# Eight weight pieces get their low half from GpSimd's subtraction instead of an accumulating transfer, and builds of one-hot sets are charged anew

## The chip, the cores and the metric

The kernel runs on one core of a Trainium2 chip. A core has five engines that run their own instruction lists in order and wait for each other through semaphores: TensorE (PE, with its weight loads shown as PEld), VectorE (DVE), ScalarE (ACT), GpSimd (POOL) and SyncE (SP), which here only issues transfers. The metric is the device time of one execution in microseconds (us); lower is better. A profiled execution gives the start and the length of every instruction.

## The reference

For x of 2048 rows (tokens) by 640 columns the kernel computes a gated mix of two layers:

```python
g = sigmoid((x * gate_w).sum(-1, keepdims=True))
a = einsum("bsd,ed->bse", x, dft_hid_re)
b = einsum("bsd,ed->bse", x, dft_hid_im)
A = einsum("ts,bse->bte", dft_seq_re, a) - einsum("ts,bse->bte", dft_seq_im, b)
# B: product-key experts. q = x @ w_q, 32 heads x 2 halves of 128
# s1, s2 = scores of each half against 16 keys; the best 2 of each give 4 pairs,
# the best 2 of these name rows (16*i1 + i2) of u and v (256 x 640) and, by softmax, weights w
# B = sum over heads and the 2 picks of  w * gelu(x . u[row]) * v[row]
out = g * A + (1 - g) * B
```

All products are made as three float32r products of a high and a low half (the low half is the float32 value less its rounded high half), so each matrix that is multiplied has to be split into two tiles first.

## The kernel before

**What runs when.** TensorE works through one long list. Its backbone are 128 *pieces*: the sequence matrices `dft_seq_re` and `dft_seq_im` come as 2 x 4 *chunks* of 512 output rows, each of 16 pieces of 128x512. Piece n is multiplied with the 128 rows `X[s]` of x (5 column blocks d, 3 matmuls each, so 15 matmuls; `seq_piece`, L146 to L148). A chunk's five banks are copied out by ScalarE (L248), multiplied by the gate on VectorE (`gate_piece`, L220) and stored. Pieces 0 to 63 are the real part, 64 to 127 the imaginary one. Between the pieces stand the score products of the expert layer (up to piece 61), the expert blocks (below), and behind piece 127 the 84 steps of the last stage.

**How a piece is split.** `split_piece(n)` is called three pieces ahead, into one of four places of the tile `WS`. ScalarE rounds the loaded piece `wf` to the high half (L141 or L191). The low half comes in one of two ways. In the first, GpSimd subtracts: low = wf - high (L142). In the second, ScalarE writes minus the high half into the low half's place (L192), and GpSimd issues a transfer that reads the piece from memory again and accumulates it there (L194). The second way holds for pieces 34 to 63, and for the even ones of pieces 76 to 90, which are eight. All other pieces take the first way. The five `wf` buffers are loaded by SyncE five pieces ahead (L180). GpSimd also splits the hidden matrices into `DD` in this stretch (`split_dd`, 128x640, ten halves between pieces 72 and 94).

**The expert part.** VectorE finds the best keys of each token (`topk`, `gates`, `weights`); then `experts` turns them into tables of sums. For each of 32 sub-blocks (g, c) `build` makes a *set* of one-hot matrices `hot` with three VectorE instructions of 128x1024 in f16 (L875: two comparisons, one multiplication). `use` lets TensorE multiply a group of up to four sets, 32 small matmuls for each (L889): such a group of 128 matmuls is called a *block* here, and there are eight blocks in the program. The first matmul of each set waits for that set's third build instruction. Behind a block ScalarE masks the result (L826) and VectorE adds it up (L832). A set's place is built again once the block has read it. There are four places, later five.

**What sets the order.** The program is written out at build time. The VectorE work of the expert part comes out of a pump, `bg`: each group of three piece matmuls adds 0.95 x 0.68 us of credit (`run_bg`), and each step of the work takes its charge off. So a charge does not change how long an instruction runs; it decides behind how many piece matmuls the next step stands, and therefore where the blocks stand in TensorE's list. A build instruction is charged by L876:

```python
for o, a, b, op in ((pt, row(0), wt, OP.is_equal), (qt, row(1), wt, OP.is_equal), (pt, pt, row(2), OP.mult)):
    nc.vector.tensor_tensor(o, a, b, op=op)
    yield (0.9 if early else 1.05) + (settle() if op == OP.mult else 0.0)
```

`early` holds for pieces before 92 (NT is 16, NC is 4, so NT * (NC + 2) - 4 is 92). N0 is 30, and N1 is 66.

Of the kernel before, what the change touches and what calls it, by code (L numbers as in the profile page):

```python
# [13 lines left out]
OP = mybir.AluOpType  # L14
# [11 lines left out]
NT = S // P  # L26
NP = NT // 2
TC = 512
NC = S // TC
NPC = 2 * NC * NT  # L30
# [13 lines left out]
MS = 64 // TB  # L44
CG = P // (TB * E)
BYPASS = 4
ACCUM_END = NT * (NC + 2) - 4


class Pump:  # L50
# [59 lines left out]
def gated_mix_kernel(ctx: ExitStack, tc: tile.TileContext, xT, xn, dreT, dimT, wsre, wsim, wq, kT, uT, vv, gw, out):  # L110
# [28 lines left out]
    def split(f, h, l, eng):  # L139

        nc.scalar.activation(h, f, AF.Copy)  # L141
        eng.tensor_sub(l, f, h.bitcast(F32))  # L142
# [29 lines left out]
    N0 = 3 * NG + 6  # L172
# [11 lines left out]
    def split_piece(n):  # L184
        if n < NPC:
            psp[n] = h, l = WS[:, n % 4, 0], WS[:, n % 4, 1]
            f = pf.pop(n)
            if not N0 + 4 <= n < (4 * NT if n % 2 else ACCUM_END) or 4 * NT <= n < N1 + 10:
                split(f, h, l, nc.gpsimd)
                return  # L190
            nc.scalar.activation(h, f, AF.Copy)  # L191
            nc.scalar.activation(l, h.bitcast(F32), AF.Copy, scale=-1.0)  # L192
            w, c, s = pieces[n]
            nc.gpsimd.dma_start(l, (wsre, wsim)[w][c, s], accum_op=OP.add)  # L194
# [7 lines left out]
    def follow(n):  # L202
        for f in then.pop(n, ()):
            f()
# [3 lines left out]
    p3, last_part, ending, closing, early, late, share = None, False, False, False, True, False, 0.95  # L208
# [22 lines left out]
    def seq_piece(n):  # L231
        w, c, s = pieces[n]
        if s == 0:
            banks[:] = [bank(d) for d in range(KD)]
        load_piece(n + 5)
        split_piece(n + 3)
        h, l = psp.pop(n)
        if n < BYPASS:
            for a, (x, c) in enumerate(((0, h), (0, l), (1, h)) if n == 0 else ((0, h), (1, h), (0, l))):
                for d in range(KD):  # L240
                    nc.tensor.matmul(banks[d], X[s][:, x, d * P:(d + 1) * P], c, start=n + a == 0, stop=False)  # L241
            return
        for d in range(KD):
            ds = slice(d * P, (d + 1) * P)
            mm3(banks[d], X[s][:, 0, ds], X[s][:, 1, ds], h, l, s == 0, s == NT - 1)
            if s == NT - 1:
                staged[n // NT, d] = f = stage()
                nc.scalar.activation(f, banks[d], AF.Copy)  # L248
            run_bg(0.68)

    for q in range(2 * NC):
        n = NT * (q + 1)
# [85 lines left out]
    for n in (1, 2):  # L338
        split_x(n)
        split_piece(n)  # L340
# [163 lines left out]
    n = b + 2  # L504
# [277 lines left out]
    for p in range(NP):  # L782
        n = N0 + 4 * p + min((p + 1) // 2, 3)
        for a in range(4):
            at(n + 1 + a, score_step, p, a)
    N1 = n + 5
# [26 lines left out]
    def experts():  # L813
# [9 lines left out]
        def mask(t):  # L823
            f = t.rearrange("p m (e t) -> p (m e) t", t=TB)
            for n in range(TB):
                nc.scalar.activation(f[:, :, n], f[:, :, n], AF.Copy, scale=mask_t[:, n:n + 1])  # L826

        def add_up(g, c, t):
            if c == 0:
                store_gates(g - 1)  # L830
                cd[g] = p3.tile([P, E, P], F32, name="cd", tag="cd")
            nc.vector.tensor_reduce(cd[g][:, :, 8 * c:8 * c + 16].rearrange("p e m -> p m e"),  # L832
                                    t.rearrange("p m (e t) -> p m e t", e=E), op=OP.add, axis=AX.X)
            if c == 14:
                summed[g] = cd[g]

        def settle(force=False):
            us = 0.0
            if masked:
                add_up(*masked.popleft())  # L840
                us = 0.75
            if unmasked and (force or not closing):
                masked.append(unmasked.popleft())
                mask(masked[-1][2])
            return us
# [16 lines left out]
        def pair(s):  # L862
            f = HOT[s][1] if s == 4 else HOT[s]
            return f[:, 0], f[:, 1]

        def build(g, c, s):
            pt, qt = (f.rearrange("p (m e t) -> p m e t", e=E, t=TB) for f in pair(s))

            def row(n):
                r = ROWS[g][:, n, 8 * c:8 * c + 8, :].rearrange("p b (s t) -> p (b s) t", t=TB)  # L870
                return r[:, :, None, :].to_broadcast(shp)

            assert rowed >= set(range(8 * g, 8 * g + 8))
            for o, a, b, op in ((pt, row(0), wt, OP.is_equal), (qt, row(1), wt, OP.is_equal), (pt, pt, row(2), OP.mult)):
                nc.vector.tensor_tensor(o, a, b, op=op)  # L875
                yield (0.9 if early else 1.05) + (settle() if op == OP.mult else 0.0)  # L876

        def use(group):
            assert not last_part
# [15 lines left out]
        while todo or prev:  # L895
            group = []
            while todo and (len(group) < (2 if ending else 4) or len(group) % 2):
                free = free_now()
                if prev and (not free or ending and any(s in (2, 3) for g, c, s in prev)):
                    yield from use(prev)  # L900
                    prev = []
                    continue
                if not free:
                    break
                s = min(free) if ending else free[0]
                free_sets.remove(s)
                g, c = todo.popleft()
                group.append((g, c, s))
                yield from build(g, c, s)
            if prev:  # L910
                if not group:
                    yield 2.2
                yield from use(prev)
            prev = group
# [165 lines left out]
    for k, (n, m) in enumerate(((-1, 2), (0, 4), (5, 7), (7, 9), (10, 12))):  # L1080
        n, m = NT * (NC + 2) + n, NT * (NC + 2) + m
# [8 lines left out]
    def split_step(m):  # L1090
        if m < 2 * NSTEP:
            b, (u, k) = m // NSTEP, divmod(m % NSTEP, KZ)
            what = UNITS[u]
            key = (b, "s" if (b or k == KD) and what in ("s1", "s2", "s4") else what, k)
            sp[m] = ring(m)[:, 0], ring(m)[:, 1]
            split(raw[key], *sp[m], nc.vector if what in ("s2", "s3") else nc.gpsimd)
            bg.credit -= 0.8 if what in ("s2", "s3") else 0.0
            if what in ("a22", "s3", "s4") or k < KD and (b == 0 or what in ("a11", "a12")):
                give(key)
# [161 lines left out]
    prep_split = {NPC - 4: (0,), NPC - 3: (1,), NPC - 2: (2,), NPC - 1: (3, 4)}  # L1261
    WP = None
    for n in range(N0, NPC):
        ending, closing, early, late = n >= NPC - 7, n % NT == NT - 1, n < ACCUM_END, n >= NT * (NC + 2) - 10
        assert n < NT * (NC + 2) - 1 or not HOT[4:] or HOT[4][0] or 4 in free_sets
        seq_piece(n)
        follow(n)
        if n >= N1 and p3 is None and NT // NB - 1 in gated:
            p2_stack.close()
            p3 = ctx.enter_context(tc.tile_pool(name="p3", bufs=1, reuse_waits="tile"))  # L1270
            pools.append(p3)
            for t in ("hot0", "WP"):
                f = p3.tile([P, 2, 2, 16 * E * 4], F16, name="hot", tag=t)
                HOT.extend(f[:, a] for a in range(2))
            bg.add(experts(), late=True)
            bg.credit -= 3.0
        if n == NPC - 4:
            bg.drain(lambda: {2, 3} <= set(free_sets))
            HOT[2:4] = None, None
            WP = p3.tile([P, 2, 2, TC], F32R, name="WP", tag="WP")  # L1280
        for m in prep_split.get(n, ()):
            split_step(m)
# [54 lines left out]
```

## Time and profile before

| what | value |
|---|---|
| median of 3 runs | 749.75 us (749.32 to 749.88) |
| the profiled execution | 750.07 us, of which its span (first to last instruction) is 748.3 us |
| VectorE busy | 577.6 us (77%) |
| GpSimd busy | 345.1 us (46%) |
| ScalarE busy | 336.8 us (45%) |
| subtractions of pieces on GpSimd, L142 WS<-wf | 89, mean 1481 ns |
| accumulating transfers, L194 | 30 of the real part, 8 of the imaginary part; these 8 land 6.1 us after issue in the median |
| granted TensorE clock | 1.0 throughout |

A row of the timeline reads: start in us, length in us, engine, line of the kernel, operation, written tile <- read tiles, shapes, count. Rows of one line that follow each other are merged (x2), and a bracket at the end gives idle time of the engine just ahead and what ended it. A row of the waits reads: who waited, for whom, us in total, times, longest.

### The profile page before, as it was taken

What the parts mean: (1) busy time and instruction counts of PE and PEld (TensorE: products, weight loads), DVE (VectorE), ACT (ScalarE), POOL (GpSimd) and SP (SyncE); (2) the same over time, 40 slices, a digit from 0 to 9 for tenths busy, and PEclk for the clock granted to TensorE, in tenths of its full rate; (3) what the DMA queues carried; (4) which work ended last, traced back from release to release, by engine and by line L of the source; (5) the groups of instructions that cost most, each with busy time, mean ns of one, the idle gap of its engine ahead of it and who ended that gap; (6) DMA issues with size and microseconds to landing.
All of it is one profiled execution on the core that took longest, in us unless ns stands there. A gap on an engine that the chain in (4) does not pass through costs nothing.

```text
span 748.3 us, 12035 instructions
## 1 busy us (share of the span) xinstructions
PE 744.0 (99%) x4437; PEld 605.2 (81%) x4437; DVE 577.6 (77%) x722; ACT 336.8 (45%) x564; POOL 345.1 (46%) x286
## 2 busy tenths in 40 slices
PE   9999999999999999999999999999999999999998
PEld 7777777888888888888888887888888888888887
DVE  6874087595999899999999978987798883357651
ACT  4335234543544745555553574422334553443351
POOL 5543323640532424145245566634356693487253
PEclk9999999999999999999999999999999999999999
DMA  9999899788566686972498766388856788875302
GB/s 336 375 387 359 332 354 387 207 233 263 143 177 136 184 232 164 243 214 71 114 393 294 157 168 197 122 291 268 272 211 197 230 260 309 246 237 175 112 29 71
DMA packets 84491, 171.17 MB, mean 229 GB/s; under 512 B 16080, under 2 KB 21328, under 8 KB 84176
## 3 DMA queue, kind: packets, MB, share of 16 engines
q1 hardware_dynamic: 76000, 155.31, 61.4%
q0 software_dynamic: 5472, 9.96, 8.5%
q10 hardware_dynamic: 2960, 5.13, 1.9%
q8 instruction: 35, 0.57, 0.3%
q14 instruction: 24, 0.20, 0.1%
HBM read 136.40 MB, written 32.39 MB: 226 GB/s over the span
## 4 chain that ended last, share of the span: by engine, by line
PE 97%; DMA 1%; issue 0%; ACT 0%; POOL 0%; DVE 0%; ACTq 0%; POOLq 0%
PE b L146 31%; PE b L147 30%; PE b L148 30%; PE b L386 2%; PE b L241 2%; PE b L889 1%; DMA WS<-in_wsim 1%; PE b L332 1%; ACT rows L730 0%; POOL DD L142 0%; ACT b L826 0%; ACT DD L141 0%; DVE ST L1222 0%; ACT WS L141 0%; ACTq L141 0%
## 5 line engine op out<-in xcount | busy, mean ns | idle before, releaser
L146 PE MATMUL b<-WS,X 128*128 128x512 f32 x620 | 243.3, 392 | 0.0
L147 PE MATMUL b<-WS,X 128*128 128x512 f32 x620 | 241.7, 390 | 0.2 <-DMA WS<-in_wsim 0.2
L148 PE MATMUL b<-WS,X 128*128 128x512 f32 x620 | 241.5, 390 | 0.0
L142 POOL TENSOR_TENSOR WS<-wf,WS 128x512 fp32r<-128x512 f32 x89 | 131.5, 1481 | 174.8 <-ACT WS L141 172.8
L146 PEld LDWEIGHTS b<-WS,X 128*128 128x128 f32 x620 | 116.4, 188 | 28.1 <-issue 4.1
L148 PEld LDWEIGHTS b<-WS,X 128*128 128x128 f32 x620 | 116.5, 188 | 24.3
L147 PEld LDWEIGHTS b<-WS,X 128*128 128x128 f32 x620 | 116.5, 188 | 24.1 <-DMA WS<-in_wsim 0.7
L141 ACT ACTIVATE WS<-wf 128x512 fp32r<-128x512 f32 x89 | 55.5, 627 | 109.4 <-PE b L148 70.9
L875 DVE TENSOR_TENSOR hot<-rows,wtab 128x1024 f16<-128x1024 f16 x56 | 50.6, 940 | 14.4 <-PE b L889 14.4
L142 POOL TENSOR_TENSOR xl<-xf,xh 128x640 fp32r<-128x640 f32 x16 | 26.8, 1677 | 72.5 <-ACT xh L141 72.5
L573 ACT ACTIVATE sc<-b 128x512 f32<-128x512 f32 x32 | 19.5, 610 | 79.9 <-PE b L148 76.1
L194 POOL DMA_DIRECT2D WS<-in_wsre x30 | 26.4, 879 | 59.5 <-ACT WS L192 58.2
L142 POOL TENSOR_TENSOR WS<-ra,WS 128x512 fp32r<-128x512 f32 x33 | 46.6, 1422 | 15.3 <-ACT WS L141 10.4
L141 ACT ACTIVATE WS<-ra 128x512 fp32r<-128x512 f32 x47 | 29.4, 631 | 42.7 <-PE b L148 28.5
L631 DVE TENSOR_TENSOR eq<-sc,mm 128x1024 f16<-128x1024 f32 x32 | 44.2, 1383 | 0.9
L638 DVE TENSOR_REDUCE tied<-eq 128x64 f32<-128x1024 f16 x32 | 39.0, 1219 | 0.9
L629 DVE TENSOR_REDUCE mm<-sc 128x64 f32<-128x1024 f32 x32 | 38.7, 1210 | 0.2
L142 POOL TENSOR_TENSOR WP<-ra,WP 128x512 fp32r<-128x512 f32 x13 | 19.2, 1490 | 31.0 <-ACT WP L141 30.9
L220 DVE SCALAR_TENSOR_TENSOR ST<-ST,grow 128x512 f32<-128x512 f32 x40 | 32.3, 864 | 0.6 <-ACT ST L248 0.6
L147 PE MATMUL b<-WU,xh 128*128 128x512 f32 x80 | 31.2, 389 | 0.0
L148 PE MATMUL b<-WU,xl 128*128 128x512 f32 x80 | 31.2, 389 | 0.0
L146 PE MATMUL b<-WU,xh 128*128 128x512 f32 x80 | 31.1, 389 | 0.0
(214 smaller groups left out, 1435.7 us busy)
## 6 DMA issues: line engine op xcount, KB each, us to landing
X<-xd SPq DMA_DIRECT2D x36, 640.0 KB, 6.6
wq<-in_wq SPq DMA_DIRECT2D x32, 640.0 KB, 7.8
wf<-in_wsim SPq DMA_DIRECT2D x64, 256.0 KB, 5.0
wf<-in_wsre SPq DMA_DIRECT2D x63, 256.0 KB, 6.7
pd<-ST SPq DMA_DIRECT2D x40, 256.0 KB, 6.1
ra<-pd SPq DMA_DIRECT2D x40, 256.0 KB, 3.5
WS<-in_wsre POOLq DMA_DIRECT2D x30, 256.0 KB, 6.3
xd<-X SPq DMA_DIRECT2D x11, 640.0 KB, 9.1
```

The costliest lines, as they stand in the source:

```text
L141: nc.scalar.activation(h, f, AF.Copy)
L142: eng.tensor_sub(l, f, h.bitcast(F32))
L146: nc.tensor.matmul(o, wh, ah, start=first, stop=False, skip_group_check=more)
L147: nc.tensor.matmul(o, wh, al, start=False, stop=False, skip_group_check=more)
L148: nc.tensor.matmul(o, wl, ah, start=False, stop=last, skip_group_check=more)
L194: nc.gpsimd.dma_start(l, (wsre, wsim)[w][c, s], accum_op=OP.add)
L220: nc.vector.scalar_tensor_tensor(f, f, -1.0 if w else 1.0, g, op0=OP.mult, op1=OP.mult)
L573: copy = lambda o, f: nc.scalar.activation(o, f, AF.Copy)
L629: nc.vector.tensor_reduce(m, sc, op=OP.max, axis=AX.X)
L631: nc.vector.tensor_tensor(eq, sc, m[:, :, None].to_broadcast([P, HH, E]), op=OP.is_equal)
L638: nc.vector.tensor_reduce(tied[:, s, ib, :], eq, op=OP.add, axis=AX.X)
L875: nc.vector.tensor_tensor(o, a, b, op=op)
```

## The change

Three lines differ:

```diff
-ACCUM_END = NT * (NC + 2) - 4
+ACCUM_END = NT * NC
...
-            if not N0 + 4 <= n < (4 * NT if n % 2 else ACCUM_END) or 4 * NT <= n < N1 + 10:
+            if not N0 + 4 <= n < ACCUM_END:
                 split(f, h, l, nc.gpsimd)
                 return
...
-                yield (0.9 if early else 1.05) + (settle() if op == OP.mult else 0.0)
+                yield (1.05 if early else 0.9) + (settle() if op == OP.mult else 0.0)
...
-        ending, closing, early, late = n >= NPC - 7, n % NT == NT - 1, n < ACCUM_END, n >= NT * (NC + 2) - 10
+        ending, closing, early, late = n >= NPC - 7, n % NT == NT - 1, n < NT * (NC + 2) - 4, n >= NT * (NC + 2) - 10
```

The accumulating way now ends with piece 63, so the even pieces 76 to 90 are split like the others: ScalarE's second pass and GpSimd's issue go, a subtraction on GpSimd comes. `early` still ends at piece 92, but the two charges have changed places: 1.05 before it, 0.9 behind it.

On GpSimd, at pieces 76 to 80, each issue `L194` has become a subtraction at the same place of the list (`DD` are the halves of the hidden matrices):

```order
 L142 TENSOR_TENSOR DD<-draw,DD 128x640
-L194 DMA WS<-in_wsim 128x512
-L142 TENSOR_TENSOR WS<-wf,WS 128x512
+L142 TENSOR_TENSOR WS<-wf,WS 128x512 x2
 L142 TENSOR_TENSOR DD<-draw,DD 128x640
-L194 DMA WS<-in_wsim 128x512
-L142 TENSOR_TENSOR WS<-wf,WS 128x512
-L194 DMA WS<-in_wsim 128x512
+L142 TENSOR_TENSOR WS<-wf,WS 128x512 x3
 L142 TENSOR_TENSOR DD<-draw,DD 128x640
```

Eight issues fewer and eight subtractions more stand on GpSimd's list; nothing else on it has moved.

On TensorE, the first block of expert matmuls stood inside piece 79, behind its second column block (bank b1). Before:

```order
L146 MATMUL b1_3074<-WS_90,X_579 128x512
L147 MATMUL b1_3074<-WS_90,X_579 128x512
L148 MATMUL b1_3074<-WS_90,X_579 128x512
L889 LDWEIGHTS hot_3442
L889 MATMUL b5_3561<-hot_3442 32x32
```

Now it stands behind the fifth (bank b4), at the end of piece 79:

```order
L146 MATMUL b4_3077<-WS_90,X_579 128x512
L147 MATMUL b4_3077<-WS_90,X_579 128x512
L148 MATMUL b4_3077<-WS_90,X_579 128x512
L889 LDWEIGHTS hot_3441
L889 MATMUL b5_3569<-hot_3441 32x32
```

That is 9 large matmuls later. Counted in the same way, the eight blocks stand 9, 15, 24, 30, 33, 18, 3 matmuls later and, the last, 3 matmuls earlier. The number of TensorE instructions and of blocks is the same.

On VectorE, the list up to the end of the first group of four sets is the same. Behind it comes the second group (`hot_` tiles, `rows0` the key rows of the first half of the tokens), with the gate's five instructions and the sums of the first block (its banks b5 and b6). Before:

```order
L875 TENSOR_TENSOR hot_3442<-rows0_1217,wtab_159 128x1024 x2
L875 TENSOR_TENSOR hot_3442<-hot_3442,rows0_1217 128x1024
L875 TENSOR_TENSOR hot_3443<-rows0_1217,wtab_159 128x1024
L220 SCALAR_TENSOR_TENSOR ST_68<-ST_68,grow_3541 128x512 x5
L875 TENSOR_TENSOR hot_3443<-rows0_1217,wtab_159 128x1024
L875 TENSOR_TENSOR hot_3443<-hot_3443,rows0_1217 128x1024
L832 TENSOR_REDUCE cd_3788<-b5_3561 128x16x16
L875 TENSOR_TENSOR hot_3443<-rows0_1217,wtab_159 128x1024 x2
L875 TENSOR_TENSOR hot_3443<-hot_3443,rows0_1217 128x1024
L832 TENSOR_REDUCE cd_3788<-b6_3626 128x16x16
```

Now:

```order
L875 TENSOR_TENSOR hot_3441<-rows0_1217,wtab_159 128x1024
L220 SCALAR_TENSOR_TENSOR ST_68<-ST_68,grow_3536 128x512 x5
L875 TENSOR_TENSOR hot_3441<-rows0_1217,wtab_159 128x1024
L875 TENSOR_TENSOR hot_3441<-hot_3441,rows0_1217 128x1024
L832 TENSOR_REDUCE cd_3780<-b5_3569 128x16x16
L875 TENSOR_TENSOR hot_3442<-rows0_1217,wtab_159 128x1024 x2
L875 TENSOR_TENSOR hot_3442<-hot_3442,rows0_1217 128x1024
L832 TENSOR_REDUCE cd_3780<-b6_3634 128x16x16
L875 TENSOR_TENSOR hot_3442<-rows0_1217,wtab_159 128x1024 x2
L875 TENSOR_TENSOR hot_3442<-hot_3442,rows0_1217 128x1024
```

The gate falls into the group's second set instead of its third, and both sums stand ahead of the fourth set instead of around it.

## The prediction

> **What bounds the kernel now.** I read the busy shares first, then TensorE's waits, then its list in order of time.
>
> ```profile
> span 748.3 us, 12035 instructions
> PE 744.0 (99%) x4437; PEld 605.2 (81%) x4437; DVE 577.6 (77%) x722; ACT 336.8 (45%) x564; POOL 345.1 (46%) x286
> PE 97%; DMA 1%; issue 0%; ACT 0%; POOL 0%; DVE 0%; ACTq 0%; POOLq 0%
> PE b L332 <- PEq L1329: 0.8, 1, 0.8
> PE b L147 <- DMA WS<-in_wsim: 0.2, 1, 0.2
> ```
>
> TensorE sets the end, from start to finish. A busy row can hide a wait, since the ends of matmuls are modelled; but the waits hold two lines only, the launch and one transfer. So the first question is how much that transfer costs. TensorE's timeline around it:
>
> ```profile
> 452.64 0.39 PE L146 MATMUL b<-WS,X 128*128 128x512 f32 x1
> 453.26 0.50 PE L147 MATMUL b<-WS,X 128*128 128x512 f32 x1 [0.23 <-DMA WS<-in_wsim]
> 453.60 0.40 PE L148 MATMUL b<-WS,X 128*128 128x512 f32 x1
> 453.93 1.26 PE L889 MATMUL b<-hot 128*32 128x32 f16 x128
> ```
>
> Undisturbed matmuls start 0.23 us apart (rows further down). Here the steps are 0.62 and 0.34 us: 0.39 too long while the accumulated low half was late, and 0.11 on restarting. That is 0.5 us, and it is all that this change could win on TensorE, whose number of instructions stays the same. A forecast of a large gain would need another bound, and the profile has none. So the question is what the change makes TensorE wait for.
>
> **What goes.** Eight accumulating transfers and their issues on GpSimd, and eight second passes on ScalarE. Their only visible cost is that 0.5 us: -0.5 (between 0, if another wait would take its place at once, and -0.5). ScalarE is busy for 45% and on no path, so its passes of 0.63 us count as nothing; less memory traffic counts as nothing too, since no other transfer ends a wait of TensorE.
>
> **What comes: subtractions that hold up VectorE.** The two engines get in each other's way. VectorE's and GpSimd's timelines ahead of the first expert block:
>
> ```profile
> 343.11 0.29 DVE L690 TENSOR_TENSOR rp<-tied 128x128 f16<-128x128 f32 x1
> 404.12 1.27 DVE L690 TENSOR_TENSOR lb<-tied 128x128 f16<-128x128 f32 x1
> 409.66 2.38 DVE L875 TENSOR_TENSOR hot<-rows,wtab 128x1024 f16<-128x1024 f16 x2
> 411.96 0.68 DVE L875 TENSOR_TENSOR hot<-hot,rows 128x1024 f16<-128x1024 f16 x1
> 412.56 1.28 DVE L875 TENSOR_TENSOR hot<-rows,wtab 128x1024 f16<-128x1024 f16 x2
> 414.37 2.97 DVE L875 TENSOR_TENSOR hot<-rows,wtab 128x1024 f16<-128x1024 f16 x2
> 417.26 1.78 DVE L875 TENSOR_TENSOR hot<-hot,rows 128x1024 f16<-128x1024 f16 x1
> 420.17 0.68 DVE L875 TENSOR_TENSOR hot<-hot,rows 128x1024 f16<-128x1024 f16 x1
> 421.13 1.29 DVE L875 TENSOR_TENSOR hot<-rows,wtab 128x1024 f16<-128x1024 f16 x2 [0.28 <-PE b L889]
> ```
>
> ```profile
> 400.75 0.90 POOL L194 DMA_DIRECT2D WS<-in_wsim  x1 [1.26 <-ACT WS L192]
> 403.90 1.33 POOL L142 TENSOR_TENSOR WS<-wf,WS 128x512 fp32r<-128x512 f32 x1 [2.26 <-ACT WS L141]
> 407.55 0.89 POOL L194 DMA_DIRECT2D WS<-in_wsim  x1 [0.73 <-ACT WS L192]
> 409.96 1.53 POOL L142 TENSOR_TENSOR WS<-wf,WS 128x512 fp32r<-128x512 f32 x1 [1.53 <-ACT WS L141]
> 414.30 0.88 POOL L194 DMA_DIRECT2D WS<-in_wsim  x1 [2.81 <-DMA wf<-in_wsim]
> 414.90 1.88 POOL L142 TENSOR_TENSOR DD<-draw,DD 128x640 fp32r<-128x640 f32 x1
> 416.75 1.75 POOL L142 TENSOR_TENSOR WS<-wf,WS 128x512 fp32r<-128x512 f32 x1
> 421.10 0.90 POOL L194 DMA_DIRECT2D WS<-in_wsim  x1 [2.60 <-ACT WS L192]
> 438.59 1.28 POOL L142 TENSOR_TENSOR WS<-wf,WS 128x512 fp32r<-128x512 f32 x1 [0.86 <-ACT WS L141]
> ```
>
> An undisturbed set takes 414.37 - 412.56 = 1.81 us, so 0.60 for an instruction. The one at 417.26, with a subtraction running, takes 1.78 instead of 0.68: +1.10. The small L690 at 404.12, again with one running, takes 1.27 where the row at 343.11 has 0.29: +0.98. The first four sets end at 420.17 + 0.68 = 420.85, after 11.19 us; four times 1.81 is 7.24, and the other 3.95 fall on three GpSimd instructions (409.96, 414.90, 416.75): 1.32 each. The issue L194 at 421.10 costs nothing: the two builds beside it take 1.29, like the undisturbed 1.28.
>
> Which new subtractions stand ahead of the end of that group? Those in place of the four issues at 400.75, 407.55, 414.30 and 421.10 (pieces 76 to 82). The first and the last of ScalarE's four high halves for them:
>
> ```profile
> 399.04 0.63 ACT L191 ACTIVATE WS<-wf 128x512 fp32r<-128x512 f32 x1 [2.14 <-issue]
> ...
> 419.39 0.63 ACT L191 ACTIVATE WS<-wf 128x512 fp32r<-128x512 f32 x1 [2.72 <-PE b L148]
> ```
>
> They are ready at 399.67 and 420.02, so all four subtractions can start before the group's present end at 420.85, and the last falls among builds that are late already. And VectorE has nothing to catch up with: its waits between 300 and 421 us are this one line,
>
> ```profile
> DVE xf L459 <- POOL xl L142: 0.2, 1, 0.2
> ```
>
> so every delay there reaches the last build. I take 1.10 for the two among VectorE's small instructions and 1.32 for the two among the builds: 2 x 1.10 + 2 x 1.32 = 4.84 us. The ends: only the two among the builds cost, at 1.10 (2.2 us), or all four cost their whole length, 1.53 by the row at 409.96 (6.1 us). The value lies between, nearest to what the same group pays now.
>
> By the Trainium skill (SBUF — State Buffer, Who interferes with whom), GpSimd and a VectorE instruction with two SBUF inputs exclude each other, and whichever starts first keeps the shared ports for its whole instruction. By that rule each subtraction costs up to its undisturbed 1.28 us, 5.1 in all, and the forecast would be 0.3 us later; the row at 425.53 below, where GpSimd waits through several VectorE instructions, shows that the order of service is less simple than that.
>
> **What moves: the block.** The first block now stands 9 matmuls later, because its 12 builds are charged 0.15 more each. The rows:
>
> ```profile
> 419.64 0.39 PE L148 MATMUL b<-WS,X 128*128 128x512 f32 x1
> 420.32 0.39 PE L148 MATMUL b<-WS,X 128*128 128x512 f32 x1
> 420.64 1.26 PE L889 MATMUL b<-hot 128*32 128x32 f16 x128
> 421.83 0.50 PE L146 MATMUL b<-WS,X 128*128 128x512 f32 x1
> ```
>
> Three matmuls take 0.68, so nine take 2.04. The block takes 421.83 - 420.64 = 1.19, and its last quarter, which needs the fourth set, begins 0.89 after its start: at 421.53 now, 0.68 after the set is ready, and at 423.57 with the change. The set will be ready at 420.85 + 4.84 = 425.69. TensorE waits 2.1 us, plus 0.1 to restart: **+2.2**. No wait comes below a delay of 2.04 + 0.68 = 2.72 us; the upper end, 6.1, gives +3.5.
>
> **The blocks behind it.** The second now starts at 439.07:
>
> ```profile
> 425.53 5.55 POOL L142 TENSOR_TENSOR DD<-draw,DD 128x640 fp32r<-128x640 f32 x1 [3.53 <-ACT DD L141]
> 431.05 1.74 POOL L142 TENSOR_TENSOR WS<-wf,WS 128x512 fp32r<-128x512 f32 x1
> 439.07 1.26 PE L889 MATMUL b<-hot 128*32 128x32 f16 x128
> 439.56 1.47 DVE L875 TENSOR_TENSOR hot<-rows,wtab 128x1024 f16<-128x1024 f16 x2 [3.47 <-PE b L889]
> DVE hot L875 <- PE b L889: 14.4, 5, 4.7
> ```
>
> It moves by 15 matmuls (3.4 us) and the 2.2 of the wait, so its last quarter begins at 439.07 + 3.4 + 2.2 + 0.9 = 445.6. Its builds start at 425.69: 12 builds, the gate's 5 and 2 sums are 19 x 0.60 = 11.4, and some seven GpSimd instructions in that time (pieces 83 to 87, two halves of DD) cost 7.7 at 1.10 to 9.2 at 1.32: ready at 444.8 to 446.3. From 0.8 early to 0.7 late; I take 0. The third moves by 24 matmuls (5.4), so its last quarter begins at 453.93 - 0.5 + 5.4 + 2.2 + 0.9 = 461.9; its builds start when the second block has read its first set (445.0) and need 14 x 0.60 + 6 x 1.32 = 16.3, ready at 461.3: 0. Further on no accumulating transfer is replaced, and VectorE idles up to 4.7 us for the block (last line), against blocks that stand at most 15 matmuls, 3.4 us, closer together because of the charge of 0.9: 0.
>
> **The low halves themselves** come earlier: a subtraction of 1.3 to 1.7 us takes the place of a second pass and a transfer of some 6 us, so that wait goes for good.
>
> **The sum.** -0.5 + 2.2 = +1.7 us. The profiled execution took 750.07 (748.3 of span and 1.8 around it) and becomes 751.8; it lies 0.3 above the median of 749.75, which becomes 751.5, **+0.23%**.
>
> **The rivals.**
>
> *No wait comes, and the kernel is not slower.* The row at 425.53 speaks for it: GpSimd's 1.9 us of work took 5.55 because VectorE did not let it in. If GpSimd gives way like that to the builds, the four subtractions cost VectorE less than 2.72 us and the first block waits for nothing. Against it: in the eleven microseconds before, at 409.96, 414.90 and 416.75, GpSimd went first. Time: 749.75 - 0.5 = 749.25. Chance 0.27.
>
> *Three blocks wait.* At 1.53 for each GpSimd instruction the first waits 3.5, the second some 1.0 and the third 0.5; 749.75 - 0.5 + 5.0 = 754.3. Against it: only one of the rows is so dear. Chance 0.12.
>
> *GpSimd's list gets late instead.* Piece 83's low half is ready at 431.05 + 1.74 = 432.8, and its first use comes about 9 + 45 + 1 matmuls after 421.83 (the rest of piece 79, then three pieces), at 434.4: 1.6 us of room. If GpSimd is shut out longer than the 3.7 us of the row at 425.53 while one more subtraction is queued ahead, TensorE waits for the low halves of pieces 83 to 85, 1 to 3 us: about 751.5 in all. The wait at the first block would itself give 2.2 us of room. Chance 0.08.
>
> *Late builds crowd VectorE* (0.9 from piece 92 on) and the sixth or seventh block waits up to a microsecond: 750.3. Against it: idle waits of VectorE up to 4.7 us there. Chance 0.03.
>
> **How the numbers follow.** The forecast has 0.50. Its own range is 749.9 (three of the four at 1.10) to 752.6 (all four at 1.32, and 0.7 at the second block). The range of 749.2 to 754.0 takes in the case with no wait and most of the case of three. A measurement of this kernel can tell about 0.2%, 1.5 us, from no change: faster means below 748.25, slower above 751.25. Nothing in the profile could bring more than 0.5 us, so faster has 0.03. Within: the case of no wait (0.27), the late builds (0.03) and of the forecast the part with a delay under 4.6 us (0.10): 0.40. Slower: 0.57.
>
> **What would show it.** Right: TensorE waits for `hot` L875 for about 2 us some 3 us after the place of the first block, and nowhere else; the line for WS<-in_wsim is gone; GpSimd has eight subtractions of 128x512 more; the first four sets take 15 us or so from the same start or a start that is 1 to 2 us later. Wrong: the first four sets end before 423.6, or TensorE's waits name `WS` L142 or a later block.

## The result, and the profile after

| | before | after |
|---|---|---|
| median of 6 runs | 749.81 us (749.32 to 750.32) | 753.5 us (752.12 to 754.68) |
| ratio of the times | | 1.0049, 95% interval 1.0034 to 1.0065 |
| the profiled execution | 750.07 us, span 748.3 | 752.12 us, span 750.2 |

The change makes the kernel 0.5% slower. The six times after lie in two groups, 752.1 to 752.6 and 754.4 to 754.7; the median falls between them, and the profiled execution belongs to the lower group. So two questions stand: what costs the lower group its 2.6 us (752.4 - 749.8), and what the other 2 us are in the upper one.

The page after, with the head, the busy shares, the chain and the group of the subtractions, in that order:

```profile
span 750.2 us, 12025 instructions
...
PE 743.5 (99%) x4437; PEld 604.7 (81%) x4437; DVE 582.1 (78%) x722; ACT 332.7 (44%) x556; POOL 344.5 (46%) x286
...
PE 71%; DVE 21%; issue 3%; SPq 2%; DMA 1%; POOL 1%; ACT 0%; DVEq 0%; POOLq 0%
...
L142 POOL TENSOR_TENSOR WS<-wf,WS 128x512 fp32r<-128x512 f32 x97 | 141.9, 1466 | 188.2 <-ACT WS L141 178.4
```

TensorE's busy time has not grown (743.5 for 744.0) and eight subtractions more stand on GpSimd (97 for 89), as the change says. The chain that ended last was 97% TensorE; now 21% of it runs through VectorE, so somewhere TensorE waited for it. TensorE's waits after name the place:

```profile
PE b L889 <- DVE hot L875: 2.6, 2, 1.9
PE b L332 <- PEq L1329: 0.8, 1, 0.8
```

The line for WS<-in_wsim is gone. Two waits for `hot` have come, and TensorE's timeline shows them at the first and at the second block:

```profile
422.21 0.97 PE L889 MATMUL b<-hot 128*32 128x32 f16 x96
423.91 0.38 PE L889 MATMUL b<-hot 128*32 128x32 f16 x32 [0.73 <-DVE hot L875]
424.22 0.50 PE L146 MATMUL b<-WS,X 128*128 128x512 f32 x1
...
442.81 1.09 PE L889 MATMUL b<-hot 128*32 128x32 f16 x96
445.75 0.38 PE L889 MATMUL b<-hot 128*32 128x32 f16 x32 [1.85 <-DVE hot L875]
446.05 0.50 PE L146 MATMUL b<-WS,X 128*128 128x512 f32 x1
```

In each block three sets run at once and the fourth is late. The last quarter is due 0.89 us after the block's start: at 423.10 and at 443.70. It starts 0.8 and 2.05 us later than that. With the 0.5 us that has gone, the stretch should be 0.8 + 2.05 - 0.5 = 2.35 us longer. The rest of the difference between the two profiled executions stands at the start of the program and has nothing to do with the change. The first piece matmul, before and after (two kernels, a fence each):

```profile
18.86 0.39 PE L146 MATMUL b<-WS,X 128*128 128x512 f32 x1
```

```profile
18.38 0.39 PE L146 MATMUL b<-WS,X 128*128 128x512 f32 x1
```

The execution after was 0.48 us ahead there, and 2.35 - 0.48 = 1.9 us is the difference of the spans.

VectorE's timeline after, from its small instructions ahead of the first group to the end of the second:

```profile
399.35 1.50 DVE L659 TENSOR_TENSOR tied<-tied,first 128x256 f32<-128x256 f32 x1
...
407.49 1.44 DVE L693 COPY lb<-lb 128x256 f16<-128x256 f16 x2
...
410.10 0.77 DVE L705 TENSOR_SCALAR cc<-cc 128x128 f32<-128x128 f32 x1
...
411.89 1.28 DVE L875 TENSOR_TENSOR hot<-rows,wtab 128x1024 f16<-128x1024 f16 x2
413.10 1.78 DVE L875 TENSOR_TENSOR hot<-hot,rows 128x1024 f16<-128x1024 f16 x1
414.80 3.75 DVE L875 TENSOR_TENSOR hot<-rows,wtab 128x1024 f16<-128x1024 f16 x2
...
420.28 1.77 DVE L875 TENSOR_TENSOR hot<-hot,rows 128x1024 f16<-128x1024 f16 x1
...
423.18 0.68 DVE L875 TENSOR_TENSOR hot<-hot,rows 128x1024 f16<-128x1024 f16 x1
423.78 3.74 DVE L875 TENSOR_TENSOR hot<-rows,wtab 128x1024 f16<-128x1024 f16 x2
...
443.94 1.75 DVE L875 TENSOR_TENSOR hot<-hot,rows 128x1024 f16<-128x1024 f16 x1
```

and GpSimd's from the last new subtraction of the first group's time (piece 82) to the end of the second group's:

```profile
419.68 1.82 POOL L142 TENSOR_TENSOR WS<-wf,WS 128x512 fp32r<-128x512 f32 x1 [1.68 <-ACT WS L141]
423.62 1.65 POOL L142 TENSOR_TENSOR DD<-draw,DD 128x640 fp32r<-128x640 f32 x1 [2.12 <-ACT DD L141]
425.23 1.74 POOL L142 TENSOR_TENSOR WS<-wf,WS 128x512 fp32r<-128x512 f32 x1
428.71 1.76 POOL L142 TENSOR_TENSOR WS<-wf,WS 128x512 fp32r<-128x512 f32 x1 [1.74 <-ACT WS L141]
432.11 1.30 POOL L142 TENSOR_TENSOR WS<-wf,WS 128x512 fp32r<-128x512 f32 x1 [1.64 <-ACT WS L141]
435.37 1.57 POOL L142 TENSOR_TENSOR DD<-draw,DD 128x640 fp32r<-128x640 f32 x1 [1.96 <-ACT DD L141]
436.90 1.74 POOL L142 TENSOR_TENSOR WS<-wf,WS 128x512 fp32r<-128x512 f32 x1
438.91 1.44 POOL L142 TENSOR_TENSOR WS<-wf,WS 128x512 fp32r<-128x512 f32 x1 [0.27 <-ACT WS L141]
441.30 1.57 POOL L142 TENSOR_TENSOR DD<-draw,DD 128x640 fp32r<-128x640 f32 x1 [0.95 <-ACT DD L141]
443.35 1.79 POOL L142 TENSOR_TENSOR WS<-wf,WS 128x512 fp32r<-128x512 f32 x1 [0.49 <-ACT WS L141]
```

*First group.* It ends at 423.18 + 0.68 = 423.86 for 420.85 before, 3.0 us later in an execution that was 0.48 ahead: a delay of 3.5 us. Each of the four new subtractions costs the instruction that it meets 1.07 to 1.10 us: the rows at 413.10 and 420.28 are 1.78 and 1.77 for 0.68, and the small ones at 399.35 and 407.49 are 1.50 and 1.44 where the kernel before has 0.43 and 0.35. Two of the four thus fall ahead of the builds, which start at 411.89 for 409.66 before.

*Second group.* It is built from 423.78 to 443.94 + 1.75 = 445.69, in 21.9 us. GpSimd ran nine instructions in that time (the last nine rows). Of the 21.9 us 11.4 are the 19 instructions of VectorE; the other 10.5 fall on the nine, 1.17 each.

### The profile page after: what moved, and what is told of

Read it like the earlier page. It is cut to its first block, busy times and chain, and to the rows that moved or that the text cites. A ratio compares the mean times of both kernels' runs of the same rounds, so it can differ in the third digit from the quotient of the medians.

```text
span 750.2 us, 12025 instructions
## 1 busy us (share of the span) xinstructions
PE 743.5 (99%) x4437; PEld 604.7 (81%) x4437; DVE 582.1 (78%) x722; ACT 332.7 (44%) x556; POOL 344.5 (46%) x286
## 4 chain that ended last, share of the span: by engine, by line
PE 71%; DVE 21%; issue 3%; SPq 2%; DMA 1%; POOL 1%; ACT 0%; DVEq 0%; POOLq 0%
PE b L146 22%; PE b L147 22%; PE b L148 22%; DVE hot L875 3%; DVE eq L631 3%; PE b L386 2%; DVE tied L638 2%; DVE mm L629 2%; PE b L241 2%; DVE eq L636 2%; DMA xf<-in_xT 1%; SPq L725 1%; DVE ST L220 1%; DVE sc L634 1%; PE b L889 1%
## 5 line engine op out<-in xcount | busy, mean ns | idle before, releaser
L142 POOL TENSOR_TENSOR WS<-wf,WS 128x512 fp32r<-128x512 f32 x97 | 141.9, 1466 | 188.2 <-ACT WS L141 178.4
L141 ACT ACTIVATE WS<-wf 128x512 fp32r<-128x512 f32 x97 | 60.6, 627 | 129.5 <-PE b L148 78.4
L875 DVE TENSOR_TENSOR hot<-rows,wtab 128x1024 f16<-128x1024 f16 x56 | 52.3, 968 | 11.7 <-PE b L889 11.7
L194 POOL DMA_DIRECT2D WS<-in_wsre x30 | 26.3, 878 | 60.4 <-ACT WS L192 59.1
L220 DVE SCALAR_TENSOR_TENSOR ST<-ST,grow 128x512 f32<-128x512 f32 x40 | 34.5, 917 | 0.8 <-ACT ST L248 0.8
```

The source lines that it names most:

```text
L220: nc.vector.scalar_tensor_tensor(f, f, -1.0 if w else 1.0, g, op0=OP.mult, op1=OP.mult)
```

## The experiments

Each run is shown with its own runs of the kernel before, whose medians lay between 749.55 and 749.81. Ratios stand with their 95% intervals.

**The two parts of the change, each alone.** The first has the subtractions and the old charges:

```diff
-                yield (1.05 if early else 0.9) + (settle() if op == OP.mult else 0.0)
+                yield (0.9 if early else 1.05) + (settle() if op == OP.mult else 0.0)
```

> Only the eight subtractions, with the old charges, so every block stands where it stood before the change. Theory (the subtractions hold up VectorE's builds): the first four sets end about 3.5 us later than before, of which 0.7 is covered, so TensorE waits some 2.8 us at the first block and some 2.2 us at the second, for hot L875; about 754.5 us. Rival (the new order of the blocks makes the loss): no wait for hot, 749.3 us, since the late transfer is gone.

Measured: 753.5 us (753.22 to 754.07), ratio 1.0054 (1.0037 to 1.0071). TensorE waits for `hot`, but at the first block only:

```profile
420.16 0.68 PE L889 MATMUL b<-hot 128*32 128x32 f16 x64
422.07 0.38 PE L889 MATMUL b<-hot 128*32 128x32 f16 x32 [1.23 <-DVE hot L875]
423.88 0.41 PE L889 MATMUL b<-hot 128*32 128x32 f16 x32 [1.43 <-DVE hot L875]
424.21 0.80 PE L146 MATMUL b<-WS,X 128*128 128x512 f32 x1
424.81 0.63 PE L147 MATMUL b<-WS,X 128*128 128x512 f32 x1
```

Where the block stands as early as before, the third and the fourth set are late, and the last quarter starts 423.88 - 420.16 - 0.89 = 2.8 us after it is due. So the subtractions make the loss, and the new charge hides a part of it at the first block. Two things were not foreseen.

The first is that the second block waits for nothing. ScalarE's timeline in this kernel, and after it that of the changed kernel, suggest why:

```profile
425.90 0.60 ACT L248 ACTIVATE ST<-b 128x512 f32<-128x512 f32 x1 [5.03 <-PE b L148]
427.16 1.31 ACT L248 ACTIVATE ST<-b 128x512 f32<-128x512 f32 x2 [0.66 <-PE b L148]
428.36 0.73 ACT L141 ACTIVATE DD<-draw 128x640 fp32r<-128x640 f32 x1
```

```profile
419.60 3.32 ACT L248 ACTIVATE ST<-b 128x512 f32<-128x512 f32 x5
422.81 0.73 ACT L141 ACTIVATE DD<-draw 128x640 fp32r<-128x640 f32 x1
```

At its old place the block stands inside piece 79, and the copies of that chunk's last three banks (L248) wait behind it. While TensorE waits, ScalarE waits too, and the high half of `DD` comes 5.5 us later. GpSimd has nothing to subtract from 421.47 to 429.17, and VectorE builds in peace. At the new place the five copies are done first, GpSimd goes on, and the second group pays. This is read from the timelines; no run tests it by itself.

The second is the row at 424.81: 0.63 for a matmul that takes 0.39 elsewhere, and the next starts 0.42 us on instead of 0.23. The table by stretches (width; busy time of PE, PEld, DVE, ACT and POOL with the number of instructions; granted clock, of which 1.00 is full speed; DMA share; GB/s):

```profile
420.00:423.50 3.50, 1.21 (x98) 0.84 (x96) 3.50 (x5) 0.78 (x2) 1.47 (x1) 1.00 0.31 76
423.50:427.00 3.50, 3.12 (x39) 2.51 (x40) 3.50 (x7) 0.60 (x1) 0.00 (x0) 0.51 0.27 97
427.00:430.50 3.50, 3.50 (x17) 2.86 (x16) 3.50 (x7) 3.13 (x6) 1.33 (x1) 1.00 0.00 0
```

The clock was halved for 3.41 us, from 423.56 in the last part of the wait to 426.97, which costs up to 1.7 us more.

The other part alone is the kernel before with the charges exchanged:

```diff
-                yield (0.9 if early else 1.05) + (settle() if op == OP.mult else 0.0)
+                yield (1.05 if early else 0.9) + (settle() if op == OP.mult else 0.0)
```

> Only the charges swapped; the eight accumulating transfers stay. Theory: the blocks stand 9 to 33 matmuls later and VectorE is no slower, so TensorE waits for no set; 749.8 us, within 0.4. Rival (the order does it): a wait at the second block as in the changed kernel, 752 us or more.

Measured: 750.19 us (749.61 to 750.58), ratio 1.0007 (0.9997 to 1.0016). No wait of TensorE but the launch. The new places of the blocks cost nothing that can be measured.

**The two halves of the eight pieces.** In the kernel before, only pieces 76 to 82, or only 84 to 90, get the subtraction:

```diff
-            if not N0 + 4 <= n < (4 * NT if n % 2 else ACCUM_END) or 4 * NT <= n < N1 + 10:
+            if not N0 + 4 <= n < (4 * NT if n % 2 else ACCUM_END) or 4 * NT <= n < N1 + 18:
```

> The counterpart of the last run: only the first four of the eight pieces (76 to 82) split by GpSimd's subtraction, 84 to 90 keep their transfers, old charges. Theory (what counts is the room ahead of the block; the first block has 0.7 us): the same waits of about 3.0 us in all at the first block as with all eight subtractions under the old charges, and the clock at half for 3.4 us behind them; 753.5 us, within 0.7. Rival (each subtraction costs its share): 751.5 us.

Measured: 754.01 us (752.96 to 756.09), ratio 1.0059 (1.0037 to 1.0081). Waits of TensorE for `hot`: 2.6 us in two pieces at the first block, then again a halved clock for 3.41 us.

```diff
-            if not N0 + 4 <= n < (4 * NT if n % 2 else ACCUM_END) or 4 * NT <= n < N1 + 10:
+            if not N0 + 4 <= n < (4 * NT if n % 2 else N1 + 18) or 4 * NT <= n < N1 + 10:
```

> The kernel before, with only the last four of the eight pieces (84 to 90) split by GpSimd's subtraction; 76 to 82 keep their transfers, and the charges are the old ones. Theory (the cost hangs on the room ahead of each block): VectorE had 3.5 and 2.3 us of idle waits ahead of the second and third block, and two or three more subtractions at 1.1 fit in; the first block is untouched. No wait, and the late transfer of piece 88 is gone: 749.2 us. Rival (each subtraction costs its share of the loss, half of +3.7): 751.5 us.

Measured: 749.65 us (749.33 to 750.21), ratio 0.9996 (0.9986 to 1.0006), no wait but the launch. With the old charges it is not the number of subtractions that counts, but which of them stand ahead of the first block, for which VectorE has no room; behind it four of them cost nothing. With the new charges this does not hold: of the nine GpSimd instructions in the second group's time three are new (pieces 84, 86 and 88), and at 1.17 us each they are more than its wait of 2.05. The new charges alone bring no wait, so it takes both. No run has the new charges with one half of the subtractions, and how that wait divides between the halves is not shown.

**Is it the sharing of memory, or only that GpSimd is busy?** Here the kernel before does work that nothing uses, ahead of each of its eight transfers: two subtractions of 128x256 in one kernel, four memsets of 128x256 in the next.

```diff
+            if n >= 4 * NT:
+                for a in range(2):
+                    nc.gpsimd.tensor_sub(scr, f[:, :TC // 2], f[:, TC // 2:])
```

> The kernel before, with two added GpSimd subtractions of 128x256 into a scratch tile ahead of each of the eight accumulating transfers (they compute nothing that is used). Transfers, ScalarE's passes and the order of the blocks stay. Theory (GpSimd's reads shut VectorE out): each pair costs VectorE 1 to 2 us among the builds, and TensorE waits for hot at the first two blocks, 3 us or more in all; 753 us or more. Rival (the loss comes from the missing transfers or from the order): no wait for hot, 749.8 us.

Measured: 755.22 us (754.02 to 756.0), ratio 1.0073 (1.0057 to 1.0089). TensorE waits for `hot` in three pieces at the first block, 3.2 us in all, and the clock is halved for 3.41 us behind them; at the second block, where a wait was expected too, there is none. A build beside such a subtraction, on VectorE and on GpSimd:

```profile
420.20 1.23 DVE L879 TENSOR_TENSOR hot<-hot,rows 128x1024 f16<-128x1024 f16 x1
...
418.54 2.34 POOL L197 TENSOR_TENSOR scr<-wf 128x256 f16<-128x256 f32 x2
```

1.23 instead of 0.68: subtractions alone, with nothing else of the change, make the wait.

```diff
+            if n >= 4 * NT:
+                for _ in range(4):
+                    nc.gpsimd.memset(scr, 0.0)
```

> The same place, but four GpSimd memsets of 128x256 f16 that read nothing. Theory (it is GpSimd's reads that shut VectorE out): builds beside a memset take 0.68 us, no wait for hot; 749.8 us. Rival (any work on GpSimd does it): waits as with the dummy subtractions, 753 us or more.

Measured: 754.65 us (754.05 to 755.37), ratio 1.0067 (1.0052 to 1.0082), which was not expected. What the run was made for came all the same: no wait for `hot`, and the two comparisons that start beside memsets take 1.28 us, as two undisturbed ones do.

```profile
418.56 1.28 DVE L879 TENSOR_TENSOR hot<-rows,wtab 128x1024 f16<-128x1024 f16 x2
...
418.03 1.41 POOL L197 MEMSET scr<- 128x256 f16 x4
```

So a GpSimd instruction that reads nothing does not hold up a build, and one that reads does. The Trainium skill (SBUF — State Buffer, Who interferes with whom) says the same of VectorE instructions with two SBUF inputs, and these rows agree: 1.28 for two builds beside memsets, as undisturbed, and 1.77 instead of 0.68 for one beside a subtraction.

The time went to something else. TensorE's longest wait in this kernel:

```profile
417.98 0.79 PE L147 MATMUL b<-WS,X 128*128 128x512 f32 x1 [2.16 <-DMA WS<-in_wsim]
```

An accumulating transfer came late, and from the end of the wait on the clock was halved again for 3.41 us. Whether the memsets ahead of the issues made it late was tried by putting them behind:

```diff
             nc.gpsimd.dma_start(l, (wsre, wsim)[w][c, s], accum_op=OP.add)
+            if n >= 4 * NT:
+                for _ in range(4):
+                    nc.gpsimd.memset(scr, 0.0)
```

> The four memsets again, now behind each accumulating transfer's issue instead of ahead of it. Theory (memsets do not touch VectorE; what the last run lost was a transfer that came late): no wait for hot, and waits for WS<-in_wsim of less than 1 us in all; 750.0 us, within 0.6. Rival (extra work on GpSimd costs TensorE in any place): 752 us or more.

Measured: 749.92 us (749.31 to 754.16), ratio 1.0009 (0.9996 to 1.0022). No wait for `hot`; one for a transfer, 1.1 us, a little more than expected, and no halved clock in the profiled execution while TensorE has matmuls left. One of the ten runs took 754.16, with a mean granted clock of 0.998. A build that lies wholly beside the memsets, on VectorE and on GpSimd:

```profile
421.94 0.68 DVE L879 TENSOR_TENSOR hot<-hot,rows 128x1024 f16<-128x1024 f16 x1
...
421.17 1.76 POOL L198 MEMSET scr<- 128x256 f16 x4
```

It takes its undisturbed 0.68. A GpSimd that is busy without reading costs nothing that can be measured here. With the memsets ahead of the issues a transfer came 2.2 us late and with them behind none by more than 1.1, but why it came late is not shown.

**Giving the builds more room.** If the loss is only that blocks stand too early for their sets, a larger charge takes it back. The changed kernel with a larger early charge:

```diff
-                yield (1.05 if early else 0.9) + (settle() if op == OP.mult else 0.0)
+                yield (1.25 if early else 0.9) + (settle() if op == OP.mult else 0.0)
```

> The changed kernel with builds charged 1.25 instead of 1.05 before piece 92, so that the blocks stand 18, 39, 57, 60, 78, 63, 69 and 63 matmuls later than before the change, instead of 9, 15, 24, 30, 33, 18, 3 and -3. Theory (the two waits are a matter of when TensorE asks for the sets): the first block comes 2.0 us later than with the change, more than the 0.9 us it waited, the second 5.4 us later; no wait, no late transfer: 749.2 us, about 0.4 under the kernel before. Rival (the added subtractions cost in another way too): 751 us or more.

Measured: 750.85 us (749.85 to 751.42), ratio 1.0013 (1.0005 to 1.0022). The waits for `hot` are gone, with eight subtractions in place. A new one, 0.7 us, stands at the start of the last stage:

```profile
598.25 0.50 PE L146 MATMUL b<-WP,DD 128*128 128x512 f32 x1 [0.66 <-DVE cd L832]
```

The last block has moved too far, and its sums (L832) are late; that is 0.7 of the 1.2 us that this kernel is slower than the one before. So the charge behind piece 92 was lowered to 0.8, to bring the last blocks forward again:

```diff
-                yield (1.25 if early else 0.9) + (settle() if op == OP.mult else 0.0)
+                yield (1.25 if early else 0.8) + (settle() if op == OP.mult else 0.0)
```

> The changed kernel with builds charged 1.25 before piece 92 and 0.8 behind it, so that the first blocks stand 18, 39 and 57 matmuls later and the last where it stood before the change. Theory: no wait for hot at the first two blocks, as with 1.25 and 0.9, and none for the last block's sums at the start of the last stage; 749.4 us, the same as before within 0.4. Rival (builds now come too fast behind piece 92): waits for hot at the sixth or seventh block, 750.5 us or more.

Measured: 749.87 us (749.4 to 750.44), ratio 0.9999 (0.999 to 1.0008). TensorE waits for nothing but the launch, as the waits show in full:

```profile
PE b L332 <- PEq L1329: 0.8, 1, 0.8
```

The whole loss is gone, but nothing has been won: this version is level with the kernel before, and none here beats it.

**The upper group of times.** The changed kernel was run three more times, to profile an execution of the upper group.

> The changed kernel once more, for its two groups of times (752.1 to 752.6 and 754.4 to 754.7). Theory (the group is decided by TensorE's clock: where the 2 us wait at the second block lies inside one 3.4 us period of the clock's control, the next period runs at half): a profile of the upper group shows one stretch of 3.4 us at clock 0.5 just behind a wait, with 0.43 us between matmuls, and waits as long as in the lower group; a profile of the lower group shows none. Rival (the waits themselves differ): the upper group has waits 2 us longer and the clock at 1.0.

> The changed kernel again for a profile of its upper group. Theory: if its time is 754 us or more, one stretch of 3.4 us at clock 0.5 behind the wait at the second block, with waits of 0.9 and 2.0 us as in the lower group; if it is below 753 us, no such stretch. Rival: the upper group has longer waits and no stretch.

> As the run before it, once more, since a profile falls into the upper group in about every second run.

Measured: 752.27 us (751.17 to 754.59 in five runs, ratio 1.0039, 1.0024 to 1.0054), 752.59 and 752.57. All three profiles are of the lower group; they repeat the two waits to 0.1 us, and the clock is not halved in them while TensorE has matmuls left. Of 13 runs of the changed kernel four took 754.4 to 754.7, each with a mean granted clock of 0.998, and nine took 751.2 to 752.8, with 0.999 or 1.0. One stretch of 3.41 us at half clock makes 1 - 0.5 x 3.41 / 752 = 0.998 and costs up to 1.7 us. So the upper group is probably the lower one with a halved clock behind the second block's wait. No profile here shows that; it stays argued, and of the 2.1 us between the groups (754.5 - 752.4) such a stretch can explain 1.7 at most.

## Why the prediction was right, and which terms were off

The median of 753.5 lies inside the range (749.2 to 754.0), 2.0 us above the forecast of 751.5. The direction held, and so did the mechanism: subtractions hold up builds, and TensorE waits for `hot`. The places and sizes of the waits did not, and that the median still lies in the range owes something to luck. The first wait came 1.35 us shorter than the sum had it and the second 2.05 us longer, so the two errors partly cancelled; and the six runs fell three to three into the two groups. The upper group lies outside the range, and with four of its times among the six the median would have too. Over all 13 runs of the changed kernel the median is 752.59.

By the prediction's own signs the account is mixed. The line for WS<-in_wsim is gone, and the first four sets end at 423.86, not before 423.6. But a wait at a later block was named as a sign of being wrong, and the second block has one. And the first four sets took 12.0 us (411.89 to 423.86) instead of 15 or so, since 2.7 of the 3.5 us fell ahead of them.

By its steps:

- *What goes, -0.5:* right. The line for WS<-in_wsim is gone, and a span without any new wait (the kernel with charges of 1.25 and 0.8) is 747.5 for 748.3, of which 0.3 is an earlier start. That is the 0.5 us; against the spread of the runs it does not show in a median.
- *New subtractions delay VectorE until the first group ends, 4.84 us:* right mechanism, 1.35 us too much; it was 3.5. I charged 1.32 for two of the new subtractions where each cost 1.07 to 1.10: the 1.32 was a mean of three, and one of them was a half of `DD`, 128x640, beside which two builds took 2.97 for 1.28, or 1.69 more. The four new ones cost 4.35 in all. And they pushed old ones to cheaper places: the subtraction of piece 79 fell partly on a RECIPROCAL, which took its usual 0.95, and on the small instruction at 410.10 (0.77 for 0.23, so 0.54 instead of 1.10), and two that met the builds at 414.80 cost 2.47 instead of 2.79. 4.35 - 0.56 - 0.32 = 3.5.
- *Wait at the first block, +2.2 with the restart:* mis-sized, for that reason alone. It was 0.8, and 0.8 + 1.35 is the forecast's, to 0.1.
- *Second block, 0:* **the term that was furthest off.** The last quarter came due where the sum had it: 445.6, less the 1.4 us by which the first wait was over-charged and the 0.48 of the earlier start, is 443.7. The sets were later. I had counted seven GpSimd instructions in the group's time (pieces 83 to 87 and two halves of `DD`); there were nine. A third half of `DD` and piece 88 (443.35) were not in my count. Two at the mean of 1.17 are 2.3 us: without them the set would have been 0.3 us early, by this estimate. The wait was 2.05.
- *Third block and later, 0:* right; no wait there.
- *The sum:* -0.5 + 0.8 + 2.05 = +2.35 us where the forecast had +1.7. On the median before, 749.81, that makes 752.2, and the lower group took 752.4. The rest of the median, one more microsecond, comes from the upper group, and its likely cause, the clock, was not in the prediction at all.

The rivals. *No wait comes* fell: in the first two groups GpSimd did not give way. *Three blocks wait* was half right: two did, by the number of instructions and not by a price of 1.53. *GpSimd's list gets late* and *late builds crowd VectorE* fell: no wait names `WS` or a block behind the second.

## What to carry to other kernels

A subtraction that costs its own engine nothing is charged to the engine that reads the same memory beside it; look for the stretches where that engine has no idle time, because there they cost. With the old charges that was the first group's, with four of the eight; with the new ones the second group's as well. Count every instruction of the other engine up to the end of the group, and up to its delayed end, not to its planned one. And where a schedule is built from charges, a dearer neighbour must be answered at every place that the charge moves: 1.25 and 0.8 took back all of the loss, while with 1.05 and 0.9 the first block waited 0.8 us instead of 2.8 and the second 2.05 instead of nothing.

## What the runs showed of the hardware

*A wait of 2 us can cost the clock.* In the trace's clock records the stretches at half clock last 3.413 us and begin at whole multiples of 3.413 us behind the first rise. I counted TensorE's idle time ahead of matmuls in each such window of the 14 profiled executions, from the first piece matmul to the last of the program. In the kernel with subtractions and old charges, for example, the window from 420.15 to 423.56 holds the whole wait of 1.23 us and 1.12 us of the one of 1.43, 2.35 in all. The four windows with 1.87, 2.10, 2.35 and 2.38 us were followed by a stretch at half clock. Those with 1.59, 1.25 and less were not. The programs' ends, where TensorE has run out of work, agree: of the windows in which its last matmul ended, those with 1.92 us of idle time or more were followed by a drop, those with 1.6 or less were not. A wait of 1.85 us therefore can go unpunished when it falls on two windows, as in the profile after (1.10 and 0.75). The Trainium skill (TensorE: Matmul & The Clock Gate, Part 1) has the window of 3413 ns and the half clock, but lets it drop only after an idle window of some 3.4 us; in these runs 1.87 us, 55% of a window, was enough.

*GpSimd is not always first.* It went ahead between two instructions of VectorE as a rule, but the `DD` subtraction issued at 429.17 in the kernel with subtractions and old charges took 4.51 us, while VectorE ran the gate and five instructions behind it:

```profile
429.17 4.51 POOL L142 TENSOR_TENSOR DD<-draw,DD 128x640 fp32r<-128x640 f32 x1 [7.70 <-ACT DD L141]
```

It ends at 433.68, and the other halves of `DD` that did not have to wait took 1.57, so it got in at about 432.1. There VectorE turns to the sums, the one instruction in this stretch that reads a bank (`b`) and no other tile:

```profile
432.17 0.68 DVE L832 TENSOR_REDUCE cd<-b 128x256 f32<-128x512 f32 x1
```

The subtraction at 425.53 in the kernel before, which took 5.55, ends 1.5 us behind the start of an L832 as well (431.08, and 429.56 for L832). Why GpSimd was let in between two VectorE instructions in other places and not here could not be told from these traces.

*An accumulating transfer can start late.* In the kernel with memsets ahead of the issue, the transfer issued at 408.18 moved its first data at 413.93 by the trace's packets, 5.75 us later; in the kernel before the same transfer was issued at 407.55 and began at 410.45. What held it is not shown.
